# Attention over channels and a squared-ReLU layer on one core: softmax read off the turned scores, norms by one-column matmuls, output halves one tile apart

## The chip, the core and the metric

The kernel runs on one core of a Trainium2 chip. Its time is the device time of one execution in microseconds (us). Before the change the median of three runs is 839.95 us (839.9 to 842.5).

## What is computed

For each of four batches, q, k and v are 6080 x 256. Columns are scaled to norm one, a 256 x 256 matrix of scores is made over the 6080 rows, its softmax is taken along each row, and v is multiplied by it. The result goes through a layer of width 2048 with a squared ReLU.

```python
qn = q / (np.linalg.norm(q, axis=1, keepdims=True) + 1e-06)
kn = k / (np.linalg.norm(k, axis=1, keepdims=True) + 1e-06)
s = kn.transpose(0, 2, 1) @ qn / tau
s = s - s.max(-1, keepdims=True)
a = np.exp(s)
a /= a.sum(-1, keepdims=True) + 1e-09
x = (v @ a).reshape(24320, 256)
r = np.maximum(x @ w_in, 0.0)
out = (s_moe * (r * r) + b) @ w_out
```

tau is 1.0. Inputs and output are float32; the matmuls of the large layers run in float16.

## The kernel before, in words

**Folding.** Since v @ a @ w_in = v @ (a @ w_in), the kernel folds the softmax `a` (256 x 256) of each batch into `w_in` once and keeps the product as `wa` (256 x 2048). The rest is a two-layer network over 24320 rows. Everything that makes `wa` for one batch is in the class `Gram`.

**Gram of a batch.** The 6080 rows come in six chunks of 128 partitions x 8 rows (the last has 120 partitions). `load` (L98 to L107) issues a transfer for k and one for q on the queue of POOL (GpSimd), which also turns float32 into float16. `mm` (L124) multiplies k by q into `s_ps` in PSUM. `norm_ops` (L137) squares k on ACT (L152) and q on DVE (L149), adds the eight rows of a partition in three steps on DVE (L161, L168, L174) and adds the result to a float32 sum `acc` (L180). `finish_ops` (L185) is then: `norms` (ones times `acc` on PE, float32, L191 and L194, then a square root on ACT), `recip` (L203, L204, over 258 columns), `scores` (two scaled products out of PSUM and a row maximum), `exps`, `soft` (divide by the sum), `a_t` (four transposes on PE), and eight `fold_w` (L252), each two matmuls of 512 columns into PSUM that ACT (L257) or DVE (L259) brings to `wa`.

**Prologue.** The Gram of batch 0 runs alone. POOL issues, in this order, its twelve chunk transfers, `w_in16`, v tile 0, v tile 1, `w_out16`, v tile 2 and `w_out32` (the last two are the same weight, as float16 and as float32). A transfer waits for the eighth before it to have landed. After the six first steps of `finish_ops` come the transposes of v tile 0, the eight `fold_w`, and the transposes of v tile 1.

**Main loop.** The 24320 rows are cut in 48 groups of 512 (the last has 256), and a group in 16 steps, one for each 128 columns of the width 2048: 768 steps. In step s, `mm1(s)` does two matmuls of 512 columns into `h_ps` (L398), ACT applies ReLU into `r16` (L401), DVE squares it into `g16` (L403). Then `mm2(s - 4)` does four matmuls of 256 columns (L415): two into each of the two PSUM halves `o_ps` that belong to the group. When the 16th step of a group is through, DVE writes both halves to `o_sb` (L422, scale and add a constant row), and SP issues the output transfer. There are three buffers for halves, so a group takes two of them and the next group's first half the third; its second half goes where the older group's first half was.

**Work beside the loop.** A table `side` says after which step each other piece is put into the queues: the load of later v tiles, the transposes of a v tile (L286, copied by DVE, L288) in the step that also holds the first output matmuls of a group, the Gram of the next batch spread over the steps of the batch before, and its `finish_ops` over the last 35 of those steps. After step 1 POOL sums the 16 parts of `w_out32` for the constant row (L320); after step 12 one matmul with ones and one DVE operation finish it (L325, L326).

**Order.** Nearly all instructions are kept in program order on their engine by hand, so each engine works through its own queue in the order in which the loop emits them.

**Buffers that matter.** `h_ps` has four PSUM buffers, shared with the tiles of `finish_ops` and of the v transposes; `r16` has three, `g16` seven.

Of the kernel before, what the change touches and what calls it, by code (L numbers as in the profile page):

```python
# [16 lines left out]
def kernel(  # L17
# [12 lines left out]
    nc = tc.nc  # L30
# [7 lines left out]

    inv_tau = 1.0 / float(tau)
    LAM = 16.0  # L40
# [17 lines left out]
    sq_pool = ctx.enter_context(tc.tile_pool(name="sq_pool", bufs=2))  # L58
    sm_pool = ctx.enter_context(tc.tile_pool(name="sm", bufs=2))
# [4 lines left out]
    gpool = ctx.enter_context(tc.tile_pool(name="gpool", bufs=LAG + 3))  # L64
# [6 lines left out]

    ident16 = consts.tile([P, P], FP16)
    make_identity(nc, ident16)
    ones32 = consts.tile([P, P], FP32)
    nc.vector.memset(ones32, 1.0)
    s_bc = consts.tile([P, 1], FP32)
    nc.sync.dma_start(out=s_bc, in_=moe_s.to_broadcast((P, 1)))
    b_bc = consts.tile([P, 1], FP32)
    nc.sync.dma_start(out=b_bc, in_=moe_b.to_broadcast((P, 1)))
    s_out = consts.tile([P, 1], FP32)  # L80
    nc.vector.tensor_scalar_mul(out=s_out, in0=s_bc, scalar1=1.0 / (LAM * LAM))
# [7 lines left out]
    chunks = []  # L89
    at = 0  # L90
    while at < N:
        rows = min(P * JC, N - at)
        assert rows % JC == 0
        chunks.append((at, rows // JC))
        at += rows
    NCH = len(chunks)

    def load_chunk(b, c):  # L98
        at, np_ = chunks[c]
        kc = qk_pool.tile([P, JC, C], FP16, tag="kc", name="kc")  # L100
        qc = qk_pool.tile([P, JC, C], FP16, tag="qc", name="qc")
        for t, src in ((kc, k), (qc, q)):
            po(nc.gpsimd.dma_start(  # L103
                out=t[:np_],
                in_=src[b, at : at + np_ * JC, :].rearrange("(p j) c -> p j c", j=JC),
            ))
        return qc, kc  # L107

    class Gram:


        def __init__(self, b):
            self.b = b
            self.tiles = {}
            self.s_ps = None

        def load(self, c):
            self.tiles[c] = load_chunk(self.b, c)

        def start(self):  # L120
            self.s_ps = ps_gram.tile([P, CH, C], FP32, tag="s_ps", name="s_ps")
            self.acc = sm_pool.tile([P, 2, C], FP32, tag="acc", name="acc")

        def mm(self, c, j):  # L124
            qc, kc = self.tiles[c]
            np_ = chunks[c][1]
            for ch in range(CH):
                po(nc.tensor.matmul(  # L128
                    self.s_ps[:, ch, :],
                    kc[:np_, j, ts(ch, P)],  # L130
                    qc[:np_, j, :],
                    start=(c == 0 and j == 0 and ch == 0),
                    stop=(c == NCH - 1 and j == JC - 1 and ch == CH - 1),
                    skip_group_check=True,
                ))

        def norm_ops(self, c):  # L137

            qc, kc = self.tiles[c]
            np_ = chunks[c][1]  # L140
            st = {}

            def squares(a, h):
                def f():
                    if "sq" not in st:
                        st["sq"] = sq_pool.tile([P, 2, JC, C], FP16, tag="sq", name="sq")
                    js = slice(h * JC // 2, (h + 1) * JC // 2)
# [8 lines left out]
            def fold1(a):  # L156
                def f():
                    if "f1" not in st:
                        st["f1"] = sq_pool.tile([P, 2, JC // 2, C], FP16, tag="f1", name="f1")
                    sq = st["sq"]  # L160
                    po(nc.vector.tensor_add(  # L161
                        st["f1"][:np_, a], sq[:np_, a, : JC // 2, :], sq[:np_, a, JC // 2 :, :]))
                return f

            def fold2():
                st["f2"] = sq_pool.tile([P, 2, JC // 4, C], FP16, tag="f2", name="f2")
                f1 = st["f1"]
                po(nc.vector.tensor_add(  # L168
                    st["f2"][:np_], f1[:np_, :, : JC // 4, :], f1[:np_, :, JC // 4 :, :]))

            def fold3():
                st["f3"] = sq_pool.tile([P, 2, C], FP16, tag="f3", name="f3")
                f2 = st["f2"]
                po(nc.vector.tensor_add(st["f3"][:np_], f2[:np_, :, 0, :], f2[:np_, :, 1, :]))  # L174

            def fold4():
                if c == 0:
                    po(nc.vector.tensor_copy(out=self.acc[:np_], in_=st["f3"][:np_]))
                else:
                    po(nc.vector.tensor_add(self.acc[:np_], self.acc[:np_], st["f3"][:np_]))  # L180

            return [squares(1, 0), squares(0, 0), squares(1, 1), squares(0, 1),
                    fold1(0), fold1(1), fold2, fold3, fold4]

        def finish_ops(self):  # L185
# [3 lines left out]
            def norms():  # L189
                n_ps = ps_h.tile([P, C + CH], FP32, tag="h_ps", name="n_ps")  # L190
                po(nc.tensor.matmul(n_ps[:, :C], ones32, self.acc[:, 0, :],  # L191
                                    start=True, stop=False, skip_group_check=True))
                for ch in range(CH):
                    po(nc.tensor.matmul(n_ps[:, C + ch : C + ch + 1], self.acc[:, 1, ts(ch, P)],  # L194
                                        ones32[:, 0:1], start=False, stop=(ch == CH - 1),
                                        skip_group_check=True))
                nrm = sm_pool.tile([P, C + CH], FP32, tag="nrm", name="nrm")
# [3 lines left out]
            def recip():  # L201
                nrm = st["nrm"]
                po(nc.vector.tensor_scalar_add(out=nrm, in0=nrm, scalar1=EPS))  # L203
                po(nc.vector.reciprocal(out=nrm, in_=nrm))  # L204

            def scores():
                nrm = st["nrm"]
                st["s"] = sm_pool.tile([P, CH, C], FP32, tag="sm_s", name="sm_s")
                for ch in range(CH):
                    po(nc.vector.scalar_tensor_tensor(  # L210
                        out=st["s"][:, ch, :], in0=self.s_ps[:, ch, :],
                        scalar=nrm[:, C + ch : C + ch + 1], op0=ALU.mult,
                        in1=nrm[:, :C], op1=ALU.mult))
                st["mx"] = sm_pool.tile([P, CH], FP32, tag="mx", name="mx")
                po(nc.vector.tensor_reduce(out=st["mx"], in_=st["s"], axis=mybir.AxisListType.X,
                                           op=ALU.max, negate=True))
                if inv_tau != 1.0:
                    po(nc.vector.tensor_scalar_mul(out=st["mx"], in0=st["mx"], scalar1=inv_tau))

            def exps():  # L220
                st["e"] = sm_pool.tile([P, CH, C], FP32, tag="sm_e", name="sm_e")
                st["sum"] = sm_pool.tile([P, CH], FP32, tag="sum", name="sum_")
                for ch in range(CH):
                    po(nc.scalar.activation(
                        out=st["e"][:, ch, :], in_=st["s"][:, ch, :], func=AF.Exp,
                        bias=st["mx"][:, ch : ch + 1], scale=inv_tau,
                        accum_out=st["sum"][:, ch : ch + 1]))

            def soft():
                po(nc.vector.reciprocal(out=st["sum"], in_=st["sum"]))  # L230
                st["a"] = sm_pool.tile([P, CH, C], FP16, tag="a16", name="a16")
                for ch in range(CH):
                    po(nc.vector.tensor_scalar_mul(
                        out=st["a"][:, ch, :], in0=st["e"][:, ch, :],
                        scalar1=st["sum"][:, ch : ch + 1]))

            def a_t():
                t_ps = ps_h.tile([P, CH, CH, P], FP16, tag="h_ps", name="t_ps")
                for j in range(CH):
                    for ch in range(CH):  # L240
                        po(nc.tensor.transpose(t_ps[:, j, ch, :], st["a"][:, ch, ts(j, P)], ident16))
                st["aT"] = sm_pool.tile([P, CH, C], FP16, tag="aT", name="aT")
                po(nc.vector.tensor_copy(out=st["aT"], in_=t_ps.rearrange("p j a c -> p j (a c)")))
                self.wa = apool.tile([P, CH, Dff], FP16, tag="wa16", name="wa16")
# [3 lines left out]
            def fold_w(fo, m):  # L248
                def f():
                    wa_ps = ps_h.tile([P, NW], FP32, tag="h_ps", name="wa_ps")  # L250
                    for j in range(CH):
                        po(nc.tensor.matmul(wa_ps, st["aT"][:, j, ts(m, P)],  # L252
# [3 lines left out]
                    if m == 0:  # L256
                        po(nc.scalar.mul(out=dst, in_=wa_ps, mul=LAM))  # L257
                    else:
                        po(nc.vector.tensor_scalar_mul(out=dst, in0=wa_ps, scalar1=LAM))  # L259
                return f  # L260

            return [norms, recip, scores, exps, soft, a_t] + [
# [29 lines left out]
    grams = {b: Gram(b) for b in range(B)}  # L292
    g0 = grams[0]
    for c in range(NCH):
        g0.load(c)
    po(nc.gpsimd.dma_start(out=w_in16, in_=moe_w_in.rearrange("(co p) f -> p co f", p=P)))
    load_v(0)
    load_v(1)
    po(nc.gpsimd.dma_start(out=w_out16, in_=moe_w_out.rearrange("(fo p) d -> p fo d", p=P)))
# [173 lines left out]
```

## Time and profile before

| | |
|---|---|
| median of three runs | 839.95 us |
| the profiled execution, own time | 841.44 us |
| its span in the profile | 839.6 us |
| mean granted TensorE clock | 0.981 |
| PE busy | 764.9 us (91%) |
| DVE busy | 536.5 us (64%) |
| ACT busy | 518.3 us (62%) |
| POOL busy | 64.0 us (8%) |

PE is TensorE, PEld its weight loads, DVE VectorE, ACT ScalarE, POOL GpSimd. Lines as L415 are lines of the kernel. A row of a timeline has start (us), duration (us), engine, line, operation and tiles, number of instructions, and in brackets the idle time before it with what ended it. A row of the waits has who waited, for whom, the total (us), how often, and the longest. A row of the groups has the count, the busy time (us), the mean of one (ns) and the idle time before. The ends of matmuls in the profile are modelled: the next one starts before the end shown, so distances between starts say more than durations.

### The profile page before, as it was taken

To read this page: it belongs to the slowest core of one execution; us is meant where nothing else is said; L and a number is where in the kernel's file an instruction comes from. 1 tells how busy PE (TensorE), PEld (TensorE's weight loads), DVE (VectorE), ACT (ScalarE), POOL (GpSimd) and SP (SyncE) were. 2 spreads that over 40 slices of the span, in tenths; PEclk is the share of its full clock that TensorE was granted. 3 is DMA by queue.
4 is the path that set the end of the run, shared out by engine and by line. 5 is a ranking of instruction groups with operands and counts; after the bars stand their busy time and mean duration, and the time that the engine had idled before them with its cause. 6 is when DMAs were issued, how large, how long until landed. Compare 5 with 4: busy or idle time off the path is not lost.

```text
span 839.6 us, 14219 instructions
## 1 busy us (share of the span) xinstructions
PE 764.9 (91%) x5542; PEld 527.6 (63%) x5542; DVE 536.5 (64%) x1134; ACT 518.3 (62%) x861; POOL 64.0 (8%) x109
## 2 busy tenths in 40 slices
PE   3559999999899999999999999999999999999997
PEld 2436666666566666666567666666656766666666
DVE  4876667766656666667655666766666556555555
ACT  3345666666666666665666666666665666666665
POOL 3134000000100010001000100000000000000000
PEclk9878999999999999999999999999999999999999
DMA  8978941214436154112624435122111212211011
GB/s 160 212 163 164 198 88 50 65 38 89 95 72 132 42 114 98 38 38 69 126 58 89 109 74 117 38 65 50 38 38 53 62 38 70 46 38 58 26 47 42
DMA packets 23955, 67.37 MB, mean 80 GB/s; under 512 B 2704, under 2 KB 4880, under 8 KB 23888
## 3 DMA queue, kind: packets, MB, share of 16 engines
q0 software_dynamic: 16688, 41.56, 28.1%
q1 hardware_dynamic: 7200, 24.91, 7.6%
q8 instruction: 43, 0.70, 0.3%
q14 instruction: 24, 0.20, 0.1%
HBM read 81.00 MB, written 24.90 MB: 126 GB/s over the span
## 4 chain that ended last, share of the span: by engine, by line
PE 76%; DMA 7%; DVE 7%; ACT 4%; issue 3%; POOL 1%; POOLq 0%; ACTq 0%
PE o_ps L415 35%; PE h_ps L398 34%; DMA qc<-in_q_dram 4%; DVE o_sb L422 4%; ACT r L401 4%; PE s_ps L128 3%; DMA w_out<-in_moe_w_out_dram 3%; PE vT_ps L286 2%; DVE g L403 2%; PE wa_ps L252 1%; POOL w_out L320 1%; DVE nrm L204 1%; ACT sq L152 0%; DVE sm_s L210 0%; DVE f L161 0%
## 5 line engine op out<-in xcount | busy, mean ns | idle before, releaser
L401 ACT ACTIVATE r<-h_ps 128x512 f16<-128x512 f32 (+1 forms) x768 | 450.4, 592 | 278.6 <-PE h_ps L398 243.9
L403 DVE TENSOR_TENSOR g<-r 128x512 f16<-128x512 f16 (+1 forms) x768 | 329.8, 431 | 279.0 <-ACT r L401 271.9
L415 PE MATMUL o_ps<-w_out,g 128*128 128x256 f16 x3040 | 467.6, 274 | 40.7 <-DVE o_sb L422 37.5
L398 PE MATMUL h_ps<-vT,wa 128*128 128x512 f16 (+7 forms) x1632 | 456.3, 367 | 0.0
L415 PEld LDWEIGHTS <-g 128*128 128x128 f16 x3040 | 296.3, 98 | 235.1 <-issue 48.2
L398 PEld LDWEIGHTS <-wa 128*128 128x128 f16 x1632 | 158.8, 98 | 29.6
L128 PE MATMUL s_ps<-qc,kc 128*128 128x256 f16 (+1 forms) x384 | 71.9, 292 | 20.8 <-DMA qc<-in_q_dram 20.7
L275 POOL DMA_DIRECT2D v<-in_v_dram x48 | 25.7, 536 | 652.5 <-PE vT_ps L286 629.6
L422 DVE SCALAR_TENSOR_TENSOR o_sb<-o_ps,s_out,rowconst 128x512 f32<-128x512 f32 x95 | 66.7, 743 | 0.5 <-PE o_ps L415 0.5
L152 ACT ACTIVATE sq<-kc 128x1024 f16<-128x1024 f16 (+1 forms) x48 | 49.7, 1048 | 21.2 <-DMA kc<-in_k_dram 21.2
L128 PEld LDWEIGHTS <-kc 128*128 128x128 f16 (+1 forms) x384 | 39.7, 104 | 28.7 <-issue 12.4
L149 DVE TENSOR_TENSOR sq<-qc 128x1024 f16<-128x1024 f16 (+1 forms) x48 | 32.4, 685 | 9.4 <-DMA qc<-in_q_dram 9.4
L288 DVE COPY vT<-vT_ps 128x1024 f16<-128x1024 f16 (+1 forms) x48 | 32.8, 684 | 0.4 <-PE vT_ps L286 0.4
L161 DVE TENSOR_TENSOR f<-sq 128x1024 f16<-128x1024 f16 (+1 forms) x48 | 32.4, 685 | 0.2
L286 PE MATMUL vT_ps<-ident,v 128*128 128x128 f16 x380 | 29.4, 221 | 0.0
L286 PEld LDWEIGHTS <-v 128*128 128x128 f16 x380 | 25.4, 98 | 1.4
L252 PE MATMUL wa_ps<-w_in,aT 128*128 128x512 f16 x64 | 18.6, 392 | 0.0
L168 DVE TENSOR_TENSOR f<-f 128x1024 f16<-128x1024 f16 (+1 forms) x24 | 16.4, 685 | 0.2
L257 ACT ACTIVATE wa<-wa_ps 128x512 f16<-128x512 f32 x16 | 9.6, 597 | 7.5 <-PE wa_ps L252 7.5
L180 DVE TENSOR_TENSOR acc<-acc,f 128x512 f32<-128x512 f32 (+1 forms) x20 | 13.7, 686 | 0.2
L103 POOL DMA_DIRECT2D kc<-in_k_dram x24 | 13.3, 553 | 5.1 <-DMA kc<-in_k_dram 5.0
L103 POOL DMA_DIRECT2D qc<-in_q_dram x24 | 13.2, 551 | 4.2 <-DMA qc<-in_q_dram 3.8
(44 smaller groups left out, 94.2 us busy)
## 6 DMA issues: line engine op xcount, KB each, us to landing
out_dram<-o_sb SPq DMA_DIRECT2D x47, 512.0 KB, 2.7
v<-in_v_dram POOLq DMA_DIRECT2D x47, 256.0 KB, 4.8
kc<-in_k_dram POOLq DMA_DIRECT2D x20, 512.0 KB, 7.7
qc<-in_q_dram POOLq DMA_DIRECT2D x20, 512.0 KB, 10.1
w_out<-in_moe_w_out_dram POOLq DMA_DIRECT2D x1, 2048.0 KB, 25.5
kc<-in_k_dram POOLq DMA_DIRECT2D x4, 480.0 KB, 7.1
qc<-in_q_dram POOLq DMA_DIRECT2D x4, 480.0 KB, 9.1
w_in<-in_moe_w_in_dram POOLq DMA_DIRECT2D x1, 1024.0 KB, 23.0
```

Of the source, the lines that this page charges most:

```text
L128: po(nc.tensor.matmul(self.s_ps[:, ch, :], kc[:np_, j, ts(ch, P)], qc[:np_, j, :], start=(c == 0 and j == 0 and ch == 0), stop=(c == NCH - ...
L149: po(nc.vector.tensor_mul(st["sq"][:np_, 0, js, :], qc[:np_, js, :], qc[:np_, js, :]))
L152: po(nc.scalar.activation(out=st["sq"][:np_, 1, js, :], in_=kc[:np_, js, :], func=AF.Square))
L161: po(nc.vector.tensor_add(st["f1"][:np_, a], sq[:np_, a, : JC // 2, :], sq[:np_, a, JC // 2 :, :]))
L252: po(nc.tensor.matmul(wa_ps, st["aT"][:, j, ts(m, P)], w_in16[:, j, ds(fo * NW, NW)], start=(j == 0), stop=(j == CH - 1)))
L286: po(nc.tensor.transpose(vT_ps[:, ch, ts(j, P)], v16[:, j, ts(ch, P)], ident16))
L288: po(nc.vector.tensor_copy(out=vT[:, :, : nj * P], in_=vT_ps[:, :, : nj * P]))
L398: po(nc.tensor.matmul(dst, wa[:, ci, ts(m, P)], src, start=(ci == 0), stop=(ci == CH - 1), skip_group_check=True))
L401: po(nc.scalar.activation(out=r16[:, :n], in_=h_ps[:, :n], func=AF.Relu))
L403: po(nc.vector.tensor_mul(g16[:, :n], r16[:, :n], r16[:, :n]))
L415: po(nc.tensor.matmul(o_halves[g, j // 2][:, j % 2, :], g16[:, ts(j, P)], w_out16[:, m, :], start=(m == 0 and j % 2 == 0), stop=(m == FT - ...
L422: po(nc.vector.scalar_tensor_tensor(out=o_sb[:, 2 * h : 2 * h + 2, :], in0=o_halves.pop((g, h)), scalar=s_out, op0=ALU.mult, in1=rowconst[ ...
```

## The change

It consists of several parts:

- **Output halves one step apart.** In step s, the matmuls of the first half belong to step s - 4, those of the second half to step s - 5. Each half is written out when its own last matmul is through; the transfer follows the second. The square of step s is put into DVE's queue behind this step's write-out. `g16` gets one buffer more.
- **Chunks of batch 0.** Five of 8 rows, then one of 4 rows and two of 2 rows a partition, the last with 96 partitions.
- **Norms.** No sum `acc`: each folded chunk (the squares themselves where there are 2 rows) is multiplied, in float16, by a column of ones, one matmul for each 128 columns of k and q: 24 for a batch, 40 for batch 0. The norms are then 4 columns and no longer 258.
- **Softmax.** The scores are scaled by k's norm only and turned in float32 on PE; exp takes the turned scores with q's norm as its scale, subtracts no maximum, and writes float16 for `fold_w`. The row sums come from four one-column matmuls, and their reciprocal is the scale with which `wa` leaves PSUM.
- **w_out.** Only the float32 copy is loaded, in two halves ahead of v tile 1; DVE and ACT make the float16 copy in eight parts after the folding and the steps 0 to 6. The sum for the constant row is done on DVE, in eight pieces after the steps 8 to 15, its matmul after step 16.
- **Prologue.** Identities and constants stand behind POOL's transfers; a first square root stands at the start. The transposes of v tile 1 move from the prologue to step 4. `finish_ops` takes 31 steps instead of 35.

The core of the diff:

```diff
-    po(nc.gpsimd.dma_start(out=w_out16, in_=moe_w_out.rearrange("(fo p) d -> p fo d", p=P)))
...
+    for h in range(2):
+        po(nc.gpsimd.dma_start(out=w_out32[:, ts(h, FT // 2), :], in_=w_out_rows[:, ts(h, FT // 2), :]))
...
+    chunks_first = make_chunks([JC] * whole + [4, 2, 2])
+    chunks_later = make_chunks([JC] * (whole + 1))
...
+                for i, (t, np_, j, a, ch) in enumerate(todo):
+                    po(nc.tensor.matmul(n_ps[:, a, ch : ch + 1], t[:np_, a, j, ts(ch, P)],
+                                        ones16[:np_, 0:1], start=(i == 0),
+                                        stop=(i == len(todo) - 1), skip_group_check=True))
...
+                po(nc.vector.tensor_mul(
+                    st["s"], self.s_ps, st["r"][:, 1, :, None].broadcast_to((P, CH, C))))
...
+                        po(nc.tensor.transpose(
+                            st["t"][:, j, ts(ch, P)], st["s"][:, ch, ts(j, P)], ident32))
...
+                    po(nc.scalar.activation(
+                        out=st["e"][:, j, :], in_=st["t"][:, j, :], func=AF.Exp,
+                        scale=st["r"][:, 0, j : j + 1]))
...
+                        po(nc.tensor.matmul(r_ps[:, ch : ch + 1], st["e"][:, j, ts(ch, P)],
+                                            ones16[:, 0:1], start=(ch == 0 and j == 0),
+                                            stop=(ch == CH - 1 and j == CH - 1),
+                                            skip_group_check=True))
...
-                        po(nc.scalar.mul(out=dst, in_=wa_ps, mul=LAM))
+                        po(nc.scalar.mul(out=dst, in_=wa_ps, mul=st["rs"][:, m : m + 1]))
...
-            po(nc.gpsimd.tensor_add(w_out32[:, :h, :], w_out32[:, :h, :], w_out32[:, h : 2 * h, :]))
+        po(nc.vector.tensor_add(w[:, a], w[:, a], w[:, b]))
...
+    for i in range(1, 8):
+        at_step(i - 1, lambda i=i: cast_w_out(i))
...
-    for s in range(NS + LAG):
-        if s < NS:
-            mm1(s)
-        if s >= LAG:
-            mm2(s - LAG)
+    for s in range(NS + LAG + 1):
+        made = mm1(s) if s < NS else None
+
+        if 0 <= s - LAG < NS:
+            mm2(s - LAG, 0)
+        if 0 <= s - LAG - 1 < NS:
+            mm2(s - LAG - 1, 1)
+        if made:
+            square(s, *made)
```

More of the change, by code (lines that the diff above doesn't have):

```diff
@@ L39 @@
     inv_tau = 1.0 / float(tau)
+    assert 0.0 < inv_tau <= 4.0
     LAM = 16.0
@@ L176, in fold4 @@
[L176 to L183, printed above, removed]
+                        st["f", half][:np_, arrays], src[:np_, arrays, :half, :],
+                        src[:np_, arrays, half : 2 * half, :]))
@@ new lines, in f, with unfolded @@
+                    if last:
+                        self.rows.append((st["f", half], np_, 1))
+                return f
+            def unfolded():
+                self.rows.append((st["sq"], np_, jc))
+            ops = []
+            for h in range(0, jc, 4):
+                js = slice(h, min(h + 4, jc))
+                ops += [squares(1, js), squares(0, js)]
+            if jc == 2:
+                return ops + [unfolded]
+            if jc == 8:
+                ops += [fold(4, slice(0, 1), False), fold(4, slice(1, 2), False)]
@@ L220, in exps @@
[L220 to L235, printed above, removed]
@@ L289, in transpose_v @@
         vT_tiles[g] = vT
-    grams = {b: Gram(b) for b in range(B)}
+    grams = {b: Gram(b, chunks_first if b == 0 else chunks_later) for b in range(B)}
     g0 = grams[0]
-    for c in range(NCH):
+    for c in range(len(g0.chunks)):
         g0.load(c)
```

243 lines of the change are left out of this document (127 added, 116 removed).

## The prediction

> **What bounds the kernel now.** I read the page first: span, busy shares, and the span in slices.
>
> ```profile
> span 839.6 us, 14219 instructions
> ...
> PE 764.9 (91%) x5542; PEld 527.6 (63%) x5542; DVE 536.5 (64%) x1134; ACT 518.3 (62%) x861; POOL 64.0 (8%) x109
> ...
> PE   3559999999899999999999999999999999999997
> ```
>
> PE is the bound from the fourth slice on, and 839.6 - 764.9 = 74.7 us of it are idle. Next the waits, which say what ended PE's idle time:
>
> ```profile
> PE o_ps L415 <- DVE o_sb L422: 37.5, 46, 2.0
> ...
> PE s_ps L128 <- DMA qc<-in_q_dram: 20.7, 6, 11.1
> ...
> PE t_ps L241 <- DVE a L233: 6.0, 1, 6.0
> ```
>
> Half of it is one wait, once for each group: the output matmuls wait for DVE to empty an output half. The rest is the prologue. Third, the loop by its chain of work and its timeline, in a stretch without a Gram:
>
> ```profile
> 662.98 0.75 DVE o_sb L422
> ...
> 815.29 0.75 DVE o_sb L422
> ```
>
> ```profile
> 770.29 0.74 DVE L422 SCALAR_TENSOR_TENSOR o_sb<-o_ps,s_out,rowconst 128x512 f32<-128x512 f32 x1
> 770.42 0.38 PE L415 MATMUL o_ps<-w_out,g 128*128 128x256 f16 x2 [0.83 <-DVE o_sb L422]
> ...
> 771.29 0.69 DVE L288 COPY vT<-vT_ps 128x1024 f16<-128x1024 f16 x1
> ...
> 772.82 0.59 PE L398 MATMUL h_ps<-vT,wa 128*128 128x512 f16 x2
> ...
> 773.45 0.60 ACT L401 ACTIVATE r<-h_ps 128x512 f16<-128x512 f32 x1 [0.27 <-PE h_ps L398]
> ...
> 774.08 0.43 DVE L403 TENSOR_TENSOR g<-r 128x512 f16<-128x512 f16 x1 [0.44 <-ACT r L401]
> ...
> 774.56 0.59 PE L398 MATMUL h_ps<-vT,wa 128*128 128x512 f16 x2
> ```
>
> ```profile
> 195.16 0.45 PE vT_ps L286 x8
> 195.61 0.43 PE h_ps L398 x2
> 196.04 0.44 PE o_ps L415 x4
> ...
> 202.56 0.43 PE n_ps L191 x2
> 202.99 0.34 PE n_ps L194 x4
> ```
>
> Two steps take 774.56 - 772.82 = 1.74 us, one 0.87 (0.43 for `h_ps`, 0.44 for `o_ps`). A group that never waits is 16 x 0.87 + 0.45 = 14.37 us. The ten groups between the first two rows took (815.29 - 662.98)/10 = 15.23. So the wait costs 0.86 us a group; its idle time (0.83) understates it a little, since the ends of matmuls are modelled.
>
> **Part 1: the halves one step apart.** Today PE has 0.22 + 0.43 + 0.22 = 0.87 us between the last matmul of a group's first half (each pair takes half of 0.44) and the next use of that buffer. In it the result must reach DVE (about 0.4 us, as from the second `h_ps` matmul, 772.82 + 0.22, to the ReLU at 773.45), the square queued ahead must end (0.43), and the half be written out (0.74). That is 1.6 us, hence the wait of about 0.8. After the change the buffer is needed a step later, and the transposes come in between: 0.87 + 0.87 + 0.45 = 2.2 us, and the square stands behind the write-out: 0.4 + 0.74 = 1.14 us. About one microsecond is to spare. What is late next is DVE: in the two steps at a boundary it has two write-outs (1.4), the copy (0.69) and two squares (0.86), 2.95 us in 1.74 + 0.45 = 2.19, so it falls 0.76 behind. Behind the write-outs are queued the squares, for which ReLU (by the three `r16`) and `mm2` wait. A square ends 774.51 - 772.82 = 1.69 us after its step began and is needed for `mm2` 4 x 0.87 + 0.43 = 3.91 after it: 2.2 us of slack. By `r16` it is 773.45 + 3 x 0.87 - 774.51 = 1.55 us. Both cover 0.76. Gain: 46 x 0.86 = 39.6 us.
>
> At three boundaries the wait is the longest of all (2.0 us), because `finish_ops` stands just ahead of it on DVE:
>
> ```profile
> 206.85 1.77 DVE L204 RECIPROCAL nrm<-nrm 128x258 f32<-128x258 f32 x1
> ...
> 211.31 1.40 DVE L422 SCALAR_TENSOR_TENSOR o_sb<-o_ps,s_out,rowconst 128x512 f32<-128x512 f32 x2
> 212.11 0.38 PE L415 MATMUL o_ps<-w_out,g 128*128 128x256 f16 x2 [2.03 <-DVE o_sb L422]
> ```
>
> The reciprocal of 258 columns becomes one of 4, and `acc` and the maximum go. That excess, 3 x (2.03 - 0.83) = 3.6 us, goes too. Together 43.2 us.
>
> **Part 2: prologue up to the first step.**
>
> ```profile
> 18.68 0.72 POOL L296 DMA_DIRECT2D w_in<-in_moe_w_in_dram  x1 [1.91 <-DMA kc<-in_k_dram]
> ...
> 21.21 0.57 POOL L275 DMA_DIRECT2D v<-in_v_dram  x1 [1.81 <-DMA qc<-in_q_dram]
> ...
> 35.62 1.29 DVE L149 TENSOR_TENSOR sq<-qc 120x1024 f16<-120x1024 f16 x2 [0.32 <-DMA qc<-in_q_dram]
> ...
> 39.47 0.69 DVE L180 TENSOR_TENSOR acc<-acc,f 120x512 f32<-120x512 f32 x1
> ...
> 48.43 1.06 PE L286 MATMUL vT_ps<-ident,v 128*128 128x128 f16 x8
> ...
> 49.29 4.33 PE L252 MATMUL wa_ps<-w_in,aT 128*128 128x512 f16 x16
> ...
> 53.91 2.32 PE L398 MATMUL h_ps<-vT,wa 128*128 128x512 f16 x10
> ```
>
> ```profile
> w_in<-in_moe_w_in_dram POOLq DMA_DIRECT2D x1, 1024.0 KB, 23.0
> ```
>
> ```profile
> DMA to landing us min/median/max: 21.7/21.7/21.7
> ```
>
> The last q lands at 35.6, `w_in` at 18.68 + 23.0 = 41.7, v tile 0 (second of these two answers) at 21.21 + 21.7 = 42.9. The transfers run one behind the other, and neither the bytes ahead of these two nor their order change, so I keep these times. From the last q to the folding the chain now takes 49.29 - 35.62 = 13.7 us. After, the last chunk is a fifth as long and unfolded: one square, 8 one-column matmuls, a small root and reciprocal, one product of 512 columns (0.7, as L180), four transposes and two exps (about 1): I estimate 6 us, the end at about 42. So v tile 0 becomes the last to arrive: PE's queue has its transposes ahead of the row sums and the folding. 42.9 + 1.1 for the transposes + some 0.8 for four one-column matmuls at a low clock gives 44.8 for the first `wa_ps`, instead of 49.29. The folding then takes what it took, without the transposes of v tile 1: first step at about 49.2, instead of 53.91. Gain 4.7 us; 0.45 is given back when those transposes run in the loop. Bounds: 2 us more if v lands earlier, 5 us less if the finer transfers or the weight come late.
>
> **Part 3: first steps.**
>
> ```profile
> 55.66 11.63 DVE L403 TENSOR_TENSOR g<-r 128x512 f16<-128x512 f16 x9
> ...
> 56.59 9.26 POOL L320 TENSOR_TENSOR w_out<-w_out 128x2048 f32<-128x2048 f32 x4 [24.39 <-DMA w_out<-in_moe_w_out_dram]
> ...
> 69.73 0.60 PE L325 MATMUL rc_ps<-w_out,ones 128*128 128x256 f32 x2
> ```
>
> Nine squares take 11.63 us while POOL sums, and PE starves. From the first step to the end of the 13th (L325) it takes 69.73 - 53.91 = 15.8 us; unhindered, four steps without output and nine full ones are 4 x 0.43 + 9 x 0.87 = 9.6. The 6.2 us are regained, less what comes instead: four casts on ACT and four on DVE, and eight sums on DVE.
>
> ```profile
> L180 DVE TENSOR_TENSOR acc<-acc,f 128x512 f32<-128x512 f32 x16 | 11.0, 686 | 0.1
> ...
> L257 ACT ACTIVATE wa<-wa_ps 128x512 f16<-128x512 f32 x16 | 9.6, 597 | 7.5 <-PE wa_ps L252 7.5
> ```
>
> A sum of 512 columns is 0.69 (first row), a cast on ACT about 0.6 (second). With a square a step (0.43) DVE has 1.12 us of work in 0.87, and falls 2 us behind over the eight steps. The slack of 1.55 to 2.2 nearly covers that; I charge 1.2, and 2.5 as the upper bound. The halves of `w_out32` follow v tile 0 and are there before the casts that read them. Net gain 5.0.
>
> **Part 4: what PE does more.** Norms were 0.43 + 0.34 = 0.77 us a batch. Now 24 weight loads with one column each; the nearest row is the eight transposes in 0.45, 0.056 each, so 1.34, and four row sums are 0.22. Four float32 transposes lie between 0.22 (as float16) and 0.87 (float32 matmuls: 0.43 for 256 columns, so 0.22 for 128); they were 0.43 with the gap between them, and I take 0.6. That is 1.0 us more for each batch in the loop, 3 in all; bounds 2 and 7.
>
> The Trainium skill, TensorE: Matmul & The Clock Gate, section LDWEIGHTS, has a weight load of 128 columns at 128/1.2 = 107 ns, which speaks against the many one-column matmuls. By it the norms would be 24 x 107 = 2.6 us and the total an estimated 4 us later. The transposes' row, each with its own weight load, shows half of that, so I follow the row.
>
> **Sum.** Gains 43.2 + 4.7 + 5.0 = 52.9; losses 0.45 + 3; and 3 us that I charge for boundaries at which a Gram's squares (0.69 each on DVE) coincide with the write-outs. Net 46.4. The profiled execution's own time is 841.44, so 795.0. The median of the runs stands 1.5 below that execution, so 793.5; I say 794.
>
> **Rivals.**
>
> *The wait only moves.* If DVE, behind at each boundary, makes ReLU or `mm2` wait instead, half of the 39.6 may stay: 794 + 20 = 814. For it: DVE's share is 64% and the boundary piles up 2.95 us. Against it: the two slacks above. Chance 0.10.
>
> *The transfers hold the prologue.* More and smaller transfers, or v tile 0 later than now, undo part 2: 794 + 5 = 799. For it: nothing arrives with margin there. Chance 0.14.
>
> *The halves don't come free.* If the buffer is given back only with the group's transfer, not with its own write-out, the boundary stays: 794 + 40 = 834. Against it: at 770.42 PE went on while the second write-out still ran (770.29 + 0.74). Chance 0.02.
>
> *Slower: a denser PE loses clock.*
>
> ```profile
> 640.00:660.00 20.00, 19.29 (x169) 15.61 (x168) 11.37 (x25) 12.54 (x21) 0.53 (x1) 1.00 0.17 41
> ```
>
> PE's roughly 750 us of work grow with one over the granted clock. At 0.94 they grow by 48 us, which eats the gain; below that the kernel is slower, at 0.90 by 794 + 83 = 877. For it: PE will have nearly no gaps. Against it: in the 20 us of this row PE was busy 96% and the granted clock 1.00. Chance 0.02.
>
> On the same page, Part 1, the skill says that a limiter takes a die to 13/16 of the clock from the third core with dense matmuls on, never with one or two; by that, this rival is out on one core. No run here shows more than one core.
>
> **How the numbers follow.** The forecast has the remaining 0.72. Its own range, from the bounds (no leftover stalls -6, v earlier -2, PE's additions +4, DVE in the first steps and at boundaries +5), is 784 to 804. The prologue rival lies in it; half of the first rival is taken in by reaching to 810. Faster by over 0.3% (about what a measurement of this kernel can tell from no change): 0.96; within 0.3%: 0.02; slower: 0.02.
>
> **What would show it.** Part 1: PE's wait for `o_sb` nearly gone from the waits, group distance about 14.4 us where no Gram runs. Part 2: first `h_ps` matmul near 49, PE's transposes of v tile 0 right behind a transfer. Part 3: 13 steps in about 11 us and no 11.63 us row of squares. Part 4: one-column matmuls at about 0.06 us each, float32 transposes below 0.9 us for four. It is wrong if the distance of groups stays above 15 us, if waits for `g` or `r` take the place of those for `o_sb`, if the first step begins after 53, or if the granted clock falls.

## The result and the profile after

The changed kernel takes 783.26 us (median of four runs, 782.96 to 783.58) where the kernel before takes 841.12 on the same chip: a ratio of 0.931, with a 95% interval of 0.929 to 0.933. The forecast was 794, with a range of 784 to 810. The direction and the mechanism were right; the gain was underestimated, and the measured time lies 0.7 us below the range. The profiled execution took 782.96 us (span 781.2), so against the profiled one before (841.44) 58.5 us went where the forecast's sum had 46.4.

The page of the changed kernel, first lines and the row of PE in slices of the span:

```profile
span 781.2 us, 14420 instructions
...
PE 753.2 (96%) x5646; PEld 527.4 (68%) x5646; DVE 505.2 (65%) x1106; ACT 517.8 (66%) x858; POOL 57.2 (7%) x111
...
PE   2689999999999999999999999999999999999997
```

PE's idle time fell from 74.7 to 28.0 us, and the third slice went from 5 tenths to 8. The waits of the whole execution, first one of ACT, then those of PE:

```profile
ACT r L420 <- DVE g L427: 23.2, 46, 0.9
...
PE s_ps L120 <- DMA qc<-in_q_dram: 18.5, 5, 11.0
...
PE vT_ps L272 <- DMA v<-in_v_dram: 2.0, 1, 2.0
...
PE t_ps L208 <- DVE sm_s L201: 1.6, 1, 1.6
...
PE rc_ps L338 <- ACT r L420: 1.2, 1, 1.2
...
PE h_ps L417 <- ACT r L420: 0.6, 3, 0.2
```

The wait of 37.5 us for `o_sb` isn't there any more, and nothing took its place: the last two rows, 1.8 us, are all that this list has for PE in the loop. ReLU's wait for the squares, which would have shown a wait that moved, is shorter too. Before, its row was:

```profile
ACT r L401 <- DVE g L403: 32.6, 57, 3.7
```

The chain of work gives the distance of groups where no Gram runs (two rows with nine groups between them), and the timeline shows one boundary:

```profile
614.85 0.45 PE vT_ps L272 x8
...
743.90 0.45 PE vT_ps L272 x8
```

```profile
613.38 0.60 PE L441 MATMUL o_ps<-w_out,g 128*128 128x256 f16 x4
613.58 0.60 ACT L420 ACTIVATE r<-h_ps 128x512 f16<-128x512 f32 x1 [0.27 <-PE h_ps L417]
613.80 0.75 DVE L449 SCALAR_TENSOR_TENSOR o_sb<-o_ps,s_out,rowconst 128x512 f32<-128x512 f32 x1
613.81 0.59 PE L417 MATMUL h_ps<-vT,wa 128*128 128x512 f16 x2
...
614.88 0.75 DVE L449 SCALAR_TENSOR_TENSOR o_sb<-o_ps,s_out,rowconst 128x512 f32<-128x512 f32 x1
```

A group takes (743.90 - 614.85)/9 = 14.34 us, as the forecast's 14.37. The first half is written out from 613.80, 0.3 us after its last matmul began, while PE goes on with `h_ps` at 613.81.

Where the time came from can be read off the step at which each ReLU starts. The table has the distances in us, from the traces; `first` is the start of the first ReLU from the beginning of the span.

| steps | before | after | gain |
|---|---|---|---|
| first | 54.54 | 48.21 | 6.33 |
| 0 to 8 | 10.83 | 5.91 | 4.92 |
| 8 to 19 | 11.16 | 11.20 | -0.04 |
| 19 to 131 | 116.49 | 110.45 | 6.04 |
| 131 to 179 (`finish_ops` of batch 1) | 51.72 | 48.20 | 3.53 |
| 179 to 323 | 147.80 | 139.41 | 8.39 |
| 323 to 371 (batch 2) | 53.19 | 48.19 | 5.00 |
| 371 to 515 | 147.80 | 139.41 | 8.39 |
| 515 to 563 (batch 3) | 53.19 | 48.20 | 4.99 |
| 563 to 643 | 76.15 | 71.76 | 4.39 |
| 643 to 755 | 105.58 | 99.30 | 6.28 |
| 755 to the end | 11.14 | 10.95 | 0.19 |

In the stretches without `finish_ops` a group gains 0.86 to 0.93 us (6.04/7, 4.39/5, 6.28/7, 8.39/9); the three stretches with `finish_ops`, three groups each, gain more.

### The profile page after: what moved, and what is told of

Its sections match the earlier page's. It is cut to its first block, busy times and chain, and to the rows that moved or that the text cites. A ratio compares the mean times of both kernels' runs of the same rounds, so it can differ in the third digit from the quotient of the medians.

```text
span 781.2 us, 14420 instructions
## 1 busy us (share of the span) xinstructions
PE 753.2 (96%) x5646; PEld 527.4 (68%) x5646; DVE 505.2 (65%) x1106; ACT 517.8 (66%) x858; POOL 57.2 (7%) x111
## 4 chain that ended last, share of the span: by engine, by line
PE 93%; DMA 5%; issue 1%; ACT 1%; DVE 0%; POOL 0%; POOLq 0%
PE o_ps L441 42%; PE h_ps L417 42%; PE s_ps L120 4%; DMA qc<-in_q_dram 4%; PE vT_ps L272 3%; PE wa_ps L237 2%; DMA v<-in_v_dram 1%; ACT r L420 0%; PE n_ps L185 0%; ACT eT L214 0%; PE t_ps L208 0%; ACT L214 0%; DVE o_sb L449 0%; PE rc_ps L338 0%; POOL kc L108 0%
## 5 line engine op out<-in xcount | busy, mean ns | idle before, releaser
L427 DVE TENSOR_TENSOR g<-r 128x512 f16<-128x512 f16 (+1 forms) x768 | 321.9, 420 | 243.4 <-ACT r L420 236.6
L441 PE MATMUL o_ps<-w_out,g 128*128 128x256 f16 x3040 | 456.8, 273 | 0.0
L449 DVE SCALAR_TENSOR_TENSOR o_sb<-o_ps,s_out,rowconst 128x512 f32<-128x512 f32 x95 | 71.1, 748 | 6.4 <-PE o_ps L441 5.6
L143 ACT ACTIVATE sq<-kc 128x1024 f16<-128x1024 f16 (+3 forms) x49 | 50.0, 1031 | 21.9 <-DMA kc<-in_k_dram 18.7
L120 PEld LDWEIGHTS <-kc 128*128 128x128 f16 (+1 forms) x384 | 40.2, 106 | 26.8 <-issue 10.2
L140 DVE TENSOR_TENSOR sq<-qc 128x1024 f16<-128x1024 f16 (+3 forms) x49 | 32.6, 675 | 11.1 <-DMA qc<-in_q_dram 11.1
L156 DVE TENSOR_TENSOR f<-f 128x512 f16<-128x512 f16 (+3 forms) x47 | 25.8, 550 | 0.4
L237 PE MATMUL wa_ps<-w_in,eT 128*128 128x512 f16 x64 | 18.9, 398 | 0.0
L242 ACT ACTIVATE wa<-wa_ps,rs 128x512 f16<-128x512 f32 x16 | 11.0, 687 | 7.6 <-PE wa_ps L237 4.3
L244 DVE TENSOR_SCALAR wa<-wa_ps,rs 128x512 f16<-128x512 f32 x16 | 11.9, 745 | 1.4 <-PE wa_ps L237 1.2
## 6 DMA issues: line engine op xcount, KB each, us to landing
qc<-in_q_dram POOLq DMA_DIRECT2D x3, 480.0 KB, 10.3
```

What stands on the lines that cost most here:

```text
L120: po(nc.tensor.matmul(self.s_ps[:, ch, :], kc[:np_, j, ts(ch, P)], qc[:np_, j, :], start=(c == 0 and j == 0 and ch == 0), stop=(c == len(s ...
L140: po(nc.vector.tensor_mul(st["sq"][:np_, 0, js, :], qc[:np_, js, :], qc[:np_, js, :]))
L143: po(nc.scalar.activation(out=st["sq"][:np_, 1, js, :], in_=kc[:np_, js, :], func=AF.Square))
L156: po(nc.vector.tensor_add(st["f", half][:np_, arrays], src[:np_, arrays, :half, :], src[:np_, arrays, half : 2 * half, :]))
L237: po(nc.tensor.matmul(wa_ps, st["e"][:, j, ts(m, P)], w_in16[:, j, ds(fo * NW, NW)], start=(j == 0), stop=(j == CH - 1)))
L427: po(nc.vector.tensor_mul(g16[:, :n], r16[:, :n], r16[:, :n]))
```

## The experiments

The theory is that PE waited for a PSUM half, that the extra step hides the write-out and everything queued around it, and that the rest of the gain is the prologue and the constant row. Rivals: the order of DVE's queue and not the distance; a lighter `finish_ops`; a wait that merely moves. Each time is compared with runs of the kernel before on the same chip. Those had medians of 844.68, 842.22 and 844.62 us in the three series, so ratios are given beside times.

**e_halves: the kernel before with the halves apart.** Loop, `mm2`, `square` and the `g16` buffer as after, all else as before.

```diff
-        if s >= LAG:
-            mm2(s - LAG)
+        if 0 <= s - LAG < NS:
+            mm2(s - LAG, 0)
+        if 0 <= s - LAG - 1 < NS:
+            mm2(s - LAG - 1, 1)
+        if made:
+            square(s, *made)
```

> The kernel before with the halves one step apart and the square behind the write-out, nothing else of the change. Theory (the wait at a group's end is for the PSUM half, and the extra step hides the write-out): the group's distance without a Gram falls from 15.23 to 14.4 us and the excess at the three finish_ops goes with it, 46 x 0.86 + 3.6 = 43 us, so about 798 us. Rival (DVE falls behind and the wait only moves): half stays, about 820. The rest of the change is then worth 798 - 783 = 15 us.

796.74 us (796.43 to 797.59), ratio 0.944 (0.942 to 0.946). The row of its waits for `o_sb`:

```profile
PE o_ps L422 <- DVE o_sb L430: 1.2, 3, 0.4
```

The wait for `o_sb` falls from 37.5 to 1.2 us, and 1.2 are three times 0.4, at the old `finish_ops`. By steps it matches the changed kernel from step 19 on: 110.67, 48.06, 139.63, 48.06, 139.63, 48.05, 71.76, 99.30. So this part alone gives nearly the whole gain of the loop, the excess at `finish_ops` included, with the old reciprocal of 258 columns still in place.

**e_square: the kernel before, only the square behind the write-out.**

```diff
-            mm1(s)
+            made = mm1(s)
         if s >= LAG:
             mm2(s - LAG)
+        if made:
+            square(s, *made)
```

> The kernel before with the square put behind the write-out, halves together. Theory (the buffer is needed 0.87 us after its last matmul): the first write-out now needs 0.4 + 0.74 = 1.14 us, so about 0.3 us of the wait stay and 0.5 x 46 = 23 us go, about 818 us. Rival (the order of DVE's queue is what costs, and the distance of the halves is not needed): nearly all goes, about 801 us. Second rival (the order is worth nothing): 841 us.

809.49 us (808.48 to 810.08), ratio 0.959 (0.957 to 0.961): between the two expectations. The same row of its waits:

```profile
PE o_ps L418 <- DVE o_sb L425: 6.7, 9, 1.7
```

Nine waits are listed where there were 46, 6.7 us where there were 37.5; three of the nine, 1.7 us each, stand at the `finish_ops`. In the steps 643 to 755 it takes 100.24 us, against 105.58 before and 99.30 after. The order alone brings 5.34 of 6.28 us there, and 0.13 us a group remain (0.94/7), not the 0.27 of the buffer arithmetic (1.14 - 0.87): the write-out begins 0.3 us after its last matmul starts, not 0.4. With a Gram beside it 0.22 us remain (141.36 against 139.41 over nine groups), and at `finish_ops` 1.65 (49.84 against 48.19). The rival was mostly right for plain boundaries. It fails where DVE is loaded.

**e_together: the changed kernel with the halves together and the square ahead**, so `mm2` and the loop as before.

> The changed kernel with the halves together again and the square ahead of the write-out, all else as changed. Theory: the wait comes back at each group, 46 x 0.86 = 40 us, about 823 us; the excess at finish_ops stays away, since the reciprocal of 258 columns is gone. Rival (the gain comes from the lighter finish_ops and prologue): below 810 us.

824.59 us (823.85 to 824.89), ratio 0.977 (0.974 to 0.979). Again that row:

```profile
PE o_ps L434 <- DVE o_sb L441: 33.7, 46, 1.3
```

All 46 waits are back, 0.73 us each. The longest is 1.3 and no longer 2.0, so the lighter `finish_ops` removes part of the excess too, when nothing else does: a stretch with `finish_ops` takes 51.24 us, 3.04 above the changed kernel's, and three plain waits make 2.5 of that (146.89 against 139.41 over nine groups).

**e_ahead: the changed kernel with the square ahead of the write-out.** Only the call of `square` moves, to directly behind `mm1`.

> The changed kernel with the square ahead of the write-out, halves still one step apart. Theory: the write-out needs 1.6 us and has 2.2, so no change: 783 us, within 2. Rival (the order of the queue is what removes the wait): 0.2 to 0.5 us a group come back, 792 to 806 us.

784.55 us (784.38 to 784.72), ratio 0.929 (0.927 to 0.931), the same ratio as the changed kernel's. By steps it equals the changed kernel within 0.05 us in every stretch after the first ReLU. The two halves of part 1 do one job: the distance hides the write-out by itself, the order all but 0.13 us of it at a plain boundary (e_square), and with the distance the order is worth nothing.

**e_oldgram: the changed kernel with the old norms, softmax and `finish_ops` for the batches 1 to 3**, where `finish_ops` takes 34 steps again.

```diff
-    grams = {b: Gram(b, chunks_first if b == 0 else chunks_later) for b in range(B)}
+    grams = {b: Gram(b, chunks_first) if b == 0 else GramOld(b, chunks_later) for b in range(B)}
...
-        fin_len = 5 * 3 + 8 * 2
+        fin_len = 6 * 3 + 8 * 2
```

> The changed kernel with norms, softmax and finish_ops of the batches 1 to 3 as before (batch 0, prologue, constant row and halves stay as changed). By the forecast's terms the new finish_ops cost PE 3 us in all and save nothing else once the halves are apart, so this kernel would take 780 us. Theory after the result (the one-column matmuls are cheaper than charged, and the reciprocal of 258 columns holds up DVE, with or without the halves apart): 783 + 3 to 6, so 786 to 789 us. If the halves alone absorb the reciprocal: 782 to 784 us.

784.64 us (783.72 to 784.98), ratio 0.931 (0.928 to 0.933). From step 19 to 563 it takes 534.1 us and the changed kernel 533.8. The new norms and softmax are worth 0.3 us in the loop: neither the 3 us of cost that the forecast charged nor the 3 to 6 us of gain expected after the result. They do not speed up the loop; the halves had already covered the old ones. A stretch with `finish_ops` is even 0.13 us longer with the new ones (48.20 against 48.06), and each of the three stretches ahead of them 0.22 shorter (110.45 against 110.67, 139.41 against 139.63).

**e_poolsum: the changed kernel with the constant row's sums on POOL.**

```diff
-        po(nc.vector.tensor_add(w[:, a], w[:, a], w[:, b]))
+        po(nc.gpsimd.tensor_add(w[:, a], w[:, a], w[:, b]))
```

> The changed kernel with the eight sums for the constant row on POOL instead of DVE, in the same eight pieces after the steps 8 to 15. Theory (a sum on POOL keeps the squares on DVE from starting, as in the kernel before): the eight pieces take 9 us or more on POOL, squares stretch, and 3 to 6 us are lost, 786 to 789 us. Rival (PE starved before because the sum stood at step 1, with four steps of slack not yet built up, or because one piece was 4.5 us long; short pieces slip in between): 782 to 784 us, since DVE's own 5 us of sums are gone.

787.48 us (786.81 to 788.79), ratio 0.935 (0.932 to 0.937), 2.9 us above e_oldgram and e_whole of the same series. Two rows of its timeline, POOL's sums and a square that runs while they do:

```profile
54.30 4.19 POOL L334 TENSOR_TENSOR w_out<-w_out 128x512 f32<-128x512 f32 x3 [0.37 <-DVE w_out L326]
...
57.29 1.48 DVE L427 TENSOR_TENSOR g<-r 128x512 f16<-128x512 f16 x1
```

A square that takes 0.42 us elsewhere takes 1.48 beside POOL's sum (4.19/3 = 1.4 us). The pieces do not wait for step 8, since POOL's queue depends on the casts alone, and so the steps 0 to 8 take 9.93 us instead of 5.91. The Trainium skill, SBUF — State Buffer, section Who interferes with whom, has a rule for it: a DVE instruction with two inputs in SBUF blocks against a GpSimd instruction that reads SBUF, because its second input comes through the shared interface. The stretched squares agree with it.

**e_whole: the changed kernel with batch 0 in whole chunks.**

```diff
-    chunks_first = make_chunks([JC] * whole + [4, 2, 2])
+    chunks_first = make_chunks([JC] * (whole + 1))
```

> The changed kernel with batch 0 in whole chunks (five of 128 x 8 rows, one of 120 x 8). Theory: the fold of the last chunk adds about 3 us between the last q and the norms, but the chain ended about 1 us before v tile 0 landed, so 2 us are lost: 785 us. Rival (the transfers set the start, whatever the chain): 783 us, within 0.5.

784.54 us (783.98 to 784.83), ratio 0.931 (0.928 to 0.933): no different from e_oldgram, which has the changed prologue. The smaller chunks bring nothing that can be told from no change. The whole chunk makes the chain of norms 2.2 us longer: its exps start at 42.28 instead of 40.13 (rows below). But the folding comes behind the transposes of v tile 0, which is there at 42.10 in the changed kernel, and so it starts at 43.29 instead of 43.08.

**e_vfirst: v tile 0 ahead of `w_in`, `w_in` in two halves.**

```diff
+    load_v(0)
-    po(nc.gpsimd.dma_start(out=w_in16, in_=moe_w_in.rearrange("(co p) f -> p co f", p=P)))
-    load_v(0)
+    for h in range(2):
+        po(nc.gpsimd.dma_start(out=w_in16[:, :, ts(h, Dff // 2)], in_=w_in_rows[:, :, ts(h, Dff // 2)]))
...
-    for f in fin[:3]:
+    for f in fin[:2]:
         f()
     transpose_v(0)
```

> The changed kernel with v tile 0 loaded ahead of w_in, w_in in two halves of 1024 columns, and the transposes of v tile 0 ahead of the turn. Theory (after the change the folding waits for v tile 0, which lands last of the two): the transposes of v go under the norms, the folding starts when the exps end and the first half of w_in is there, about 41.2 instead of 43.1 us, so 1 to 2 us are gained: 781.5 to 782.3 us. Rival (two smaller transfers of w_in take longer than one, or the chain of norms is as late): 783 us or more.

781.57 us (781.53 to 782.76), ratio 0.928 (0.925 to 0.930), 3 us below its two neighbours. In its profile the first `wa_ps` matmul starts at 41.06 us; in the changed kernel it is 43.08, in the two neighbours 43.51 and 43.29. So the transfer of v tile 0 did set the start. The order is worth 2.0 to 2.5 us at this point; the first ReLU begins 1.4 us ahead of the changed kernel's (46.83 against 48.21) and 2.5 to 2.7 ahead of the neighbours', because the clock during the folding differs between profiles (last section). The changed kernel's timeline, from the exps to the first `h_ps`:

```profile
40.13 0.84 ACT L214 ACTIVATE eT<-t_ps,rnrm 128x256 f16<-128x256 f32 x2 [0.71 <-PE t_ps L208]
...
42.10 1.03 PE L272 MATMUL vT_ps<-ident,v 128*128 128x128 f16 x8 [2.00 <-DMA v<-in_v_dram]
...
43.08 4.67 PE L237 MATMUL wa_ps<-w_in,eT 128*128 128x512 f16 x16
...
47.58 2.32 PE L417 MATMUL h_ps<-vT,wa 128*128 128x512 f16 x10
```

**e_dve1 and e_dve3: the changed kernel with one or three more products on DVE at each boundary.** They go to a spare tile; three instead of one in the second.

```diff
         vT_tiles[g] = vT
+        for _ in range(1 if 3 <= g < NG - 1 else 0):
+            po(nc.vector.tensor_mul(spare, vT.rearrange("p c t -> p (c t)"), vT.rearrange("p c t -> p (c t)")))
```

> The changed kernel with one more product of 128 x 1024 (0.69 us) on DVE behind the copy of each v tile from the fourth on; it is written to a spare tile and not used. By the slack worked out in the forecast DVE then falls 0.76 + 0.69 = 1.45 us behind at each boundary, below the 1.55 us of r16: no loss, 783 us within 1. Rival (boundaries have no slack to speak of, which is what the 3 us for leftover stalls stood for): 0.3 us or more at each of 44 boundaries, 796 us or more.

784.5 us in one run; its steps from 0 to the end equal the changed kernel's within 0.02 us in every stretch, and only the start differs (49.40 against 48.21). Nothing at all is lost at the boundaries.

> The same with three more products at each boundary. DVE falls 0.76 + 2.07 = 2.83 us behind, more than the 2.2 us until mm2 needs its square: 0.6 us lost at each of 44 boundaries, 27 us, so about 810 us, and waits of PE for g or of ReLU for g. Rival (the slack is larger, since DVE catches up 0.44 us in every step before the oldest square is needed): below 790 us.

793.26 us in one run: 10.3 us above the changed kernel by the span. It loses 0.22 us a group with a Gram (141.40 against 139.41 over nine groups), 0.1 without (100.00 against 99.30 over seven) and 0.43 at `finish_ops` (49.49 against 48.20 over three), 10.2 us from the first ReLU on where 27 were expected. So the slack is larger than the forecast's rows gave, as the rival says, though the time is not below its 790 us. The wait that appears is the expected one, of PE and its weight loads for the square:

```profile
PEld L444 <- DVE g L430: 21.3, 44, 0.8
...
PE o_ps L444 <- DVE g L430: 2.9, 11, 0.3
```

**c_after: the changed kernel again.**

> The changed kernel itself, as the measure for the three beside it: 783 us, with the start of the first step at 47 to 49.5 us by the phase in which the clock of TensorE rises.

783.17 us (783.00 to 784.58), ratio 0.929 (0.926 to 0.931), first ReLU at 48.25 us.

**e_best: e_vfirst, the sums spread, three idle matmuls.**

```diff
-    for i, (part, n) in enumerate(todo):
-        at_step(8 + i, lambda part=part, n=n: rowconst_sum(part, n))
-    at_step(8 + len(todo), rowconst_mm)
+    for step, (part, n) in zip((6, 8, 9, 11, 12, 14, 15, 17), todo):
+        at_step(step, lambda part=part, n=n: rowconst_sum(part, n))
+    at_step(18, rowconst_mm)
...
+    busy(2)
+    fin[2]()
+    busy(1)
```

> The changed kernel with v tile 0 ahead of w_in and w_in in halves (as in the earlier run), the eight sums for the constant row spread over the steps 6 to 17 and their matmul after step 18, and three matmuls of 512 columns whose result is not used in PE's idle time around the turn. Theory: 2 us from the transfers, 1 us from the sums (steps 8 to 19 in 10.2 instead of 11.2 us), and 0.5 to 1.5 us from a clock that rises before the folding: 779 us, 3 to 4 us below the changed kernel on the same chip. If the clock does not rise earlier for three matmuls: 780 us.

780.77 us (780.46 to 781.66), ratio 0.926 (0.924 to 0.928), 2.4 us below c_after of the same series and the lowest median here, though its interval overlaps e_vfirst's. The steps 8 to 19 take 10.26 us instead of 11.20, as expected for the spread sums. The first ReLU starts at 47.88 in the profile, not earlier than in e_vfirst (46.83): no gain from the idle matmuls shows. The profiled execution is the slowest of the four (781.66 us), and why its start is later is a matter of the clock (below).

## Why the prediction was right in its mechanism and short in its sum

**Part 1, the boundary, was right.** The wait for `o_sb` went from 37.5 us to nothing, e_halves alone shows it, and groups are 14.34 us apart. The term was 0.86 us a group and measured 0.86 to 0.93, some 0.9, so 46 groups are about 41.4 instead of 39.6: 1.8 us short.

**The excess at `finish_ops` was mis-sized, and its cause given too narrowly.** The forecast had 3.6 us, from the idle time (2.03 against 0.83), and gave the lighter reciprocal as the reason that it goes. e_halves removes it with the old reciprocal in place, and e_together, with the lighter one, only in part. The three stretches of e_halves (131 to 179, 323 to 371, 515 to 563) show 3.66 + 5.13 + 5.14 = 13.9 us of gain, of which nine groups at 0.9 are 8.1. The excess was 5.8 us. The part not foreseen is a drop of the granted clock behind the wait in the batches 2 and 3, before the change. The timeline of batch 2, and then the windows view of the stretch behind the wait (busy time of PE, PEld, DVE, ACT and POOL, then the granted clock, the share of the DMA engines and GB/s):

```profile
411.63 0.38 PE L415 MATMUL o_ps<-w_out,g 128*128 128x256 f16 x2 [2.03 <-DVE o_sb L422]
...
412.89 1.06 PE L415 MATMUL o_ps<-w_out,g 128*128 128x256 f16 x4
```

```profile
412.30:416.00 3.70, 3.70 (x17) 1.94 (x15) 1.31 (x3) 2.84 (x6) 1.60 (x3) 0.54 0.73 181
```

Four output matmuls that take 0.60 us at full clock take 1.06, and the granted clock over these 3.7 us is 0.54. Where the drop came, the stretch took 1.47 us more (53.19 against 51.72), 2.9 us in the two; the other 2.9 us of excess are below the 3.6 of the forecast. The trace of before held these rows; the forecast rested on the wait of batch 1 alone, behind which the granted clock was 1.00 from 212 to 216 us.

**The charge for leftover stalls is the step that failed outright.** "3 us that I charge for boundaries at which a Gram's squares coincide with the write-outs" had no row of such a stall behind it. The forecast's own arithmetic said that DVE falls 0.76 us behind and has 1.55 us of slack. e_dve1 puts 0.69 us more on every boundary from the fourth v tile on and loses nothing. That slack was there, e_dve3 shows it larger still, and the charge contradicted it.

**Part 4, what PE does more, was mis-sized.** It charged 1.0 us a batch, 3 in all; e_oldgram shows a gain of 0.3. The chain of work of the changed kernel has the price of the norms of batch 1:

```profile
187.27 0.58 PE n_ps L185 x24
187.85 0.45 PE h_ps L417 x2
```

24 one-column matmuls with their weight loads take 0.58 us, 0.024 each, not 0.056: the row of the transposes was taken as the price, but each of those also moves 128 columns. So the new norms are cheaper than the old (0.58 against 0.77). The four row sums take 0.10 us in the same way, but 0.45 up to the next `h_ps`, since PE waits there for a ReLU that stands behind the exps on ACT: these are the three waits of 0.2 us in the list after the change. The four float32 transposes take 0.44 us, not 0.6, from their start to that of the next `h_ps` in the timeline:

```profile
193.36 0.60 PE L208 MATMUL t_ps<-ident,sm_s 128*128 128x128 f32 x4
...
193.80 0.59 PE L417 MATMUL h_ps<-vT,wa 128*128 128x512 f16 x2
```

The Trainium skill, TensorE: Matmul & The Clock Gate, section Back-to-back issue gap, puts matmuls of 1 to 64 columns at an issue floor of about 25 ns, and the trace agrees. The forecast weighed the page's figure for weight loads (107 ns) and left this one out, which would have given 24 x 25 = 0.6 us.

**Part 2, the prologue, was right in what sets it.** v tile 0 is the last to arrive, e_vfirst starts the folding 2.0 to 2.5 us earlier by its order, and e_whole shows the chain of norms in front of it to be covered. The forecast of the first step was 49.2 us and it began at 47.58: v landed at 42.10 instead of 42.9, its transposes took 0.8 instead of 1.1, and the row sums, for whose 0.8 us no row stood, took 0.15. The term was 4.7 and measured 6.3. Of this difference luck may be a part: the first ReLU of e_halves and e_square, which have the prologue of before, began at 56.39 and 56.12 us and not at 54.54, and the changed prologue's varies as well (last section). Which of the other parts of the prologue (norms, softmax, constants behind the transfers) made the chain short enough was not tried apart.

**Part 3, the first steps, was right.** It had a net 5.0 us, less 0.45 for the transposes of v tile 1; the steps 0 to 19 gained 4.88. e_poolsum shows the block by POOL at 4 us in the steps 0 to 8, and e_best that 0.94 of DVE's sums could be saved (11.20 against 10.26), where 1.2 had been charged. The wait is PE's ahead of the constant row's matmul, 1.2 us in the waits above. The list names a ReLU, but the last one before it had ended at 61.27 us. The matmul reads what the last sum writes, and starts 0.1 us after its end (61.72 + 0.42); in e_best the distance is the same, and the wait 0.2 us. So the cost is the last sum's delay, where the charge was for late squares:

```profile
61.72 0.42 DVE L334 TENSOR_TENSOR w_out<-w_out 128x256 f32<-128x256 f32 x1
...
62.24 0.67 PE L338 MATMUL rc_ps<-w_out,ones 128*128 128x256 f32 x2 [1.17 <-ACT r L420]
```

**The sum.** From 46.4 to 58.5 us: 1.6 at the start, 0.3 in the first steps, 1.8 at the plain boundaries, and 8.2 at `finish_ops` and the leftovers (3 of charge without a row, some 3 of PE's additions, 2.2 of excess). All four point the same way. The range's lower end had allowed for them in part only: 6 us for leftover stalls, of which the sum had charged 3, and 2 for an earlier v, and nothing for one-column matmuls cheaper than charged or a larger excess. Its own working is off as well: 794 less these 8 is 786, not 784.

**The rivals.** The wait did not move (the rows of PE and ACT after the change), the transfers held the prologue only as forecast, the halves do come free one by one. A denser PE lost no clock: the mean granted clock was 0.986, and 0.981 before.

## What to carry to other kernels

Where PE waits at each tile's end for one engine to empty PSUM, look at what has the buffer's next turn: one step of distance, or the write-out ahead of its engine's other work, hides it. Here the distance was enough alone, and the order nearly so while that engine was lightly loaded. Let a charge in a sum have a row of its own; an allowance that contradicts the slack already worked out only spoils the sum. Once a loop's wait is covered, making lighter what stood behind it may bring nothing, as the softmax here.

## What the runs showed of the hardware

Two waits of PE of 2.0 us were followed by a granted clock of 0.54 over 3.7 us (412.30 to 416.00 and 613.70 to 617.40); a third of the same length, in batch 1, was not. Behind the three waits of 1.7 us in e_square the granted clock was 1.00. The trace of before has no other drop between 70 and 830 us, so the waits are the likely cause, but this was not tried by itself.

The start varies with the clock too. Eight of the profiles have the changed kernel's instructions up to the first ReLU. It began at 48.18 to 48.27 us in four of them (the changed kernel, c_after, e_together, e_dve3), at 49.40, 49.49 and 49.62 in three (e_dve1, e_oldgram, e_ahead), and at 50.35 in e_poolsum. From 45.4 to 47.3 us, during the folding, the granted clock was 1.00 in the first four and 0.50 in the other four. The windows view of the changed kernel, then of e_dve1:

```profile
45.40:47.30 1.90, 1.90 (x10) 0.87 (x9) 1.46 (x3) 1.37 (x2) 0.30 (x1) 1.00 1.09 261
...
45.40:47.30 1.90, 1.90 (x6) 0.61 (x5) 0.94 (x2) 0.69 (x1) 0.39 (x1) 0.50 1.09 270
```

So differences of 1 to 2 us between runs can be the start alone. The 16 folding matmuls took 4.5 us in the changed kernel and 5.6 in e_best, whose granted clock over its folding was 0.50, then 0.73 (in the changed kernel it was 0.94 in the second of these stretches):

```profile
43.00:45.00 2.00, 2.00 (x7) 0.64 (x5) 0.75 (x1) 0.98 (x2) 0.53 (x1) 0.50 1.02 406
...
45.00:47.00 2.00, 2.00 (x8) 0.81 (x7) 1.16 (x2) 0.73 (x2) 0.53 (x1) 0.73 1.07 312
```

The Trainium skill, TensorE: Matmul & The Clock Gate, Part 1, has a clock gate with two states and a free-running window of about 3.4 us; the clock falls after an idle window and rises after a busy one. The rows agree with half and full clock. A drop behind a wait of 2.0 us, shorter than such a window, is not what the page says, and here the rows decide. That it depends on where in a window a wait or the first matmuls fall would fit both, but was not tried by itself; the three matmuls that e_best puts into the idle time did not bring the clock up earlier in its profile.
